# Fused chunk-select attention and soft-slot experts: longer load runs with 64 by 64 transposes, a maximum subtracted in PSUM, and combine transposes moved

## Chip, core and metric

The kernel runs on one core of one Trainium2 chip. The metric is the device time of a launch in microseconds (us). The kernel before took 165.16 us, the median of three runs (163.99 to 166.2).

## Reference

The work is an attention over selected chunks followed by a soft mixture of experts.

```python
# q, k, v: (4, 8, 768, 64) = (batch, heads, positions, head_dim), float32
k_min, k_max = min and max of k over each chunk of 32 positions      # 24 chunks
ub = sum(maximum(q * k_min, q * k_max), axis=-1)                      # bound per query and chunk
top_chunks = argsort(where(causal, ub, -1e9))[..., -6:]
scores = q @ k.T / 8, masked to the six chunks and to j <= i
attn = softmax(scores) @ v                                            # x: (3072, 512)

logits = x @ phi                                                      # 32 slots = 8 experts x 4
d = softmax of logits over the 3072 rows                              # dispatch
slot_out[e] = relu((d.T @ x)[e] @ w1[e]) @ w2[e]                      # w1 (8,512,1024), w2 (8,1024,512)
out = softmax of logits over the 32 slots @ slot_out                  # combine, (3072, 512) float32
```

## The kernel before

The 4 batches of 8 heads are worked as 16 pairs of heads (`NPAIR`). The order of the work on every engine is written out by hand: each engine runs its instructions in the order in which the program lists them. `GpSimd` issues all loads (`load`, `load_v`, `load_w`), which also convert float32 to bfloat16; `SyncE` issues the stores of the result.

A pair of heads passes through these steps. `load` (L141) brings q or k as a tile with 128 partitions; partition p holds, for each of the two heads, 6 neighbouring positions of 64 values, that is two runs of 1.5 KB of float32. `transposes` (L203) turns it with 12 TensorE matmuls against the identity: for each of the 6 positions and each head, 128 partitions by 64 columns become 64 partitions by 128 columns, head 0 on partitions 0 to 63 of PSUM and head 1 on 64 to 127. `evac_T` (L215) copies the result to SBUF on ScalarE and puts the positions back in order. From the transposed k, VectorE takes minimum and maximum per chunk (`kmin`, `kmax`); `qsplit` splits q by sign; `ubound` forms the bounds on TensorE, `select` finds the sixth largest on VectorE, and `ns_transposes` turns the selection. `scores` (L294) forms the scores of both heads, `expo` (L318) takes the exponential on ScalarE, `mask` applies the causal mask on GpSimd, and `pv` multiplies with v.

The loop over pairs (L591) mixes the steps of several pairs: in round i TensorE forms the scores of pair i, the bounds of pair i + 1, the transposes of pair i + 2, the products with v of pair i - 1, and the transposes of the finished rows of pair i - 2. Three pairs of transposes stand ahead of the loop, so 13 pairs are transposed in it. After the fourth pair of a batch the soft-slot steps for that batch follow (`moe_...`): `moe_logits` (L389), the exponentials against a running maximum over the batches, `moe_dispatch` (the slots' inputs `si`), and `moe_ct` (L506), which transposes the batch's combine weights from `c_pad` into `cT_all`.

The last batch (`BL`) is worked in the open after the loop. Its logits `lg1` lie in one PSUM tile (`lgt`). The maximum over the rows is `pm`, then transposed, reduced to `mneg` (negated) and spread over the partitions again by a small float32 product `bc` (L728). `bc` is copied to SBUF (`bc_sb`), added to the logits (`ld`), and ScalarE takes the exponential `d_sb`. `moe_dispatch(BL)` follows, and its result goes to `siT_pad`, on which the first expert layer `experts_in` waits. `keep(n)` (L687) puts n filler matmuls of 480 columns, whose results are not used, into TensorE's queue. Between the two halves of the first expert layer stands `moe_ct(BL)`. `sums` (L808) forms the slots' normaliser and the column sums of the last batch's combine weights; `inv_a` and `inv_b` hold the reciprocals that scale the output rows, `zinv` the slots' one. `experts_out` and `last_expert_out` form the second layer, the last one in two halves y (`so_sb[0]`, `so_sb[1]`). The output loop (L889) forms 12 blocks of 256 rows with five buffers: one half of a block is scaled on ScalarE, one on VectorE, and SyncE stores the block.

Of the kernel before, what the change touches and what calls it, by code (L numbers as in the profile page):

```python
# [20 lines left out]
NQT = 6  # L21
# [39 lines left out]
def kernel(  # L61
# [17 lines left out]
    SPE = NS // E  # L79
    NDG, NFG = Dm // P, F // P  # L80
    EARLY = 14
    LAST = NPAIR - 1

    ctx.enter_context(tc.manual_schedule())
# [117 lines left out]

    def transposes(i, nm):  # L203

        ps = p_tp.tile([P, NQT, P], BF16, name="tr_ps", tag="tp")
        src = st.pop((nm, i))
        for g in range(NQT):
            for h in range(2):
                nc.tensor.matmul(  # L209
                    ps[h * 64:(h + 1) * 64, g, :], lhsT=src[:, h, g * D:(g + 1) * D], rhs=ident,  # L210
                    is_transpose=True,
                )
        st[nm + "ps", i] = ps

    def evac_T(i, nm):  # L215

        t = tp3.tile([P, S], BF16, name=nm + "T", tag=nm + "T")
        nc.scalar.copy(  # L218
            t.rearrange("d (p g) -> d p g", g=NQT),
            st.pop((nm + "ps", i)).rearrange("d g p -> d p g"),  # L220
        )
        st[nm + "T", i] = t
# [163 lines left out]
        copy(st["xT", b][:, j, t0 * P:t1 * P], ps[:, t0:t1].rearrange("p t c -> p (t c)"))  # L386


    def moe_logits(b, hgs=range(NDG), ps=None, last=True):  # L389
        if ps is None:  # L390
            ps = st["lgps", b] = p_tp.tile([P, NQT, NS], F32, name="lg_ps", tag="tp")
        xT = st["xT", b]
        for t in range(NQT):
            for hg in hgs:
                nc.tensor.matmul(
                    ps[:, t, :], lhsT=xT[:, hg, t * P:(t + 1) * P], rhs=phi_sb[:, hg, :],
                    start=(hg == 0 and t == 0), stop=(last and hg == NDG - 1 and t == NQT - 1),
                )

    def moe_copy(b):  # L400
# [281 lines left out]
    normalise(LAST, 0, 3, at_a)  # L682
    pv(LAST, [4, 5])
    lgt = p_at.tile([P, 2, 512], F32, name="lgt_ps", tag="at")
    lg1 = lgt[:, 0, :NQT * NS].rearrange("p (t s) -> p t s", t=NQT)

    def keep(n):  # L687
        for _ in range(n):
            nc.tensor.matmul(h_ps[0][:, 1, CH:], lhsT=ident, rhs=w_sb[0][:, CH:512], start=True, stop=True)

    moe_logits(BL, range(NDG - 1), lg1)
    x_transposes(LAST, 0, 3)
    evac_x(LAST, 0, 3, nc.scalar.copy)
    normalise(LAST, 3, NQT, at_b)
# [3 lines left out]
    def col_sums(ps, b):  # L698
        c = cT_all[:, b * NQT:(b + 1) * NQT].rearrange("p (m a) (c x) -> p m x (a c)", a=2, x=2)
        for n in range(NQT):  # L700
            nc.tensor.matmul(
                ps[:, n:n + 1], lhsT=c[:, n // 2, n % 2], rhs=live, start=True, stop=True)

    csa = h_ps[0][:, 1, :BL * NQT]
    for b in range(BL):
        col_sums(csa[:, b * NQT:(b + 1) * NQT], b)
    moe_logits(BL, range(NDG - 1, NDG), lg1)
# [12 lines left out]
    inv_a = tail.tile([P, BL * NQT], F32, name="inv_a")  # L720
    inv_b = tail.tile([P, 1 + NQT], F32, name="inv_b")

    def cinv(n):
        return inv_a[:, n:n + 1] if n < BL * NQT else inv_b[:, 1 + n - BL * NQT:2 + n - BL * NQT]

    keep(2)
    bc = p_tp.tile([P, NS], F32, name="bc_ps", tag="tp")
    nc.tensor.matmul(  # L728
        bc, lhsT=mneg.broadcast_to([NS, P]), rhs=identf[:NS, :NS], start=True, stop=True,
    )  # L730
    rm = small.tile([P, NQT, 1], F32, name="rm", tag="rm")
    nc.vector.tensor_reduce(rm, lg1, axis=AX.X, op=ALU.max)
    nc.vector.reciprocal(inv_a, csa)
    bc_sb = small.tile([P, 1, NS], F32, name="bc_sb", tag="bc_sb")
    nc.vector.tensor_copy(bc_sb[:, 0, :], bc)
    ld = small.tile([P, NQT, NS], F32, name="ld", tag="ld")
    nc.vector.tensor_tensor(ld, lg1, bc_sb.broadcast_to([P, NQT, NS]), op=ALU.add)
    d_sb = small.tile([P, NQT, NS], BF16, name="d_sb", tag="d_sb")
    nc.scalar.activation(d_sb, ld, func=ACT.Exp)
    st["d", BL] = d_sb  # L740
    dm = small.tile([P, 1, NS], F32, name="dm", tag="dm")
    nc.vector.tensor_tensor(dm, m_old.rearrange("p (o s) -> p o s", o=1), bc_sb, op=ALU.add)
# [26 lines left out]
    for g in range(2):  # L769
# [8 lines left out]
    zinv = inv_b[:, :1]  # L778
# [29 lines left out]
    def sums():  # L808
        ps = p_tp.tile([P, 1 + NQT], F32, name="z_ps", tag="tp")
        nc.tensor.matmul(  # L810
            ps[:, :1], lhsT=zrow.rearrange("p j s -> p (j s)"), rhs=identf[:1, :1], start=True, stop=True)
        col_sums(ps[:, 1:], BL)
        nc.vector.reciprocal(inv_b, ps)

    HD = Dm // 2
# [23 lines left out]
            )  # L839

    experts_in(0, 0)
    moe_ct(B - 1)
    experts_in(0, 1)
    relu(0)
    experts_in(1, 0)
# [6 lines left out]
    def rows(m):  # L852
        return out[m * 2 * P:(m + 1) * 2 * P, :].rearrange("(p x) d -> p x d", x=2)
# [14 lines left out]
    nc.vector.tensor_scalar_mul(so_part, so_ps[:, HD:], zinv)  # L868
# [32 lines left out]


# [28 lines left out]
```

## Time and profile before

| | |
|---|---|
| median of three runs | 165.16 us |
| profiled execution | 164.61 us, span 162.9 us |
| TensorE busy | 140.9 us (86%) |
| VectorE busy | 123.3 us (76%) |
| ScalarE busy | 122.3 us (75%) |
| GpSimd busy | 103.2 us (63%) |
| HBM read, written | 52.49 MB, 6.29 MB |
| mean granted TensorE clock | 0.953 |

The profile is of one execution. Times in the timeline are in us from the start of the span. A row of the timeline has the start, the time, the engine, the line of the kernel, the operation, the tiles that it writes and reads, their shapes, and how many instructions were merged; in square brackets stands how long the engine was idle before, and what ended that. PE is TensorE's matmuls, PEld its weight loads, DVE is VectorE, ACT ScalarE, POOL GpSimd and SP SyncE. The chain is the work that ended last, followed back from the last instruction; its rows have start, time and work. The strips divide the span in 40 slices, with the busy share in tenths. Matmuls are pipelined, and their ends in the trace are modelled.

### The profile page before, as it was taken

The page shows a single profiled execution, that of the slowest core. Times are in us where ns is not written, and L with a number is a line of the kernel's source. Part 1 is how long each engine was busy: PE and PEld are TensorE (multiplying, and loading weights), DVE is VectorE, ACT ScalarE, POOL GpSimd, SP SyncE. Part 2 cuts the span into 40 slices and gives each one's busy share as a digit, 9 for nine tenths or more (in the row PEclk, how much of TensorE's full clock was granted, in tenths as well). Part 3 has the DMA queues.
Part 4 walks back from the last instruction along what each step waited for, and adds up shares of the span by engine and source line. Part 5 has one row for each costly group of instructions (what it writes and reads, how often), then busy time and mean ns, then how long its engine had stood idle before and what let it go on. Part 6 is the DMA issues. An engine that isn't in the chain of part 4 may idle for free.

```text
span 162.9 us, 5890 instructions
## 1 busy us (share of the span) xinstructions
PE 140.9 (86%) x2417; PEld 91.6 (56%) x2417; DVE 123.3 (76%) x434; ACT 122.3 (75%) x168; POOL 103.2 (63%) x203
## 2 busy tenths in 40 slices
PE   7796779999999999999999899998989899986600
PEld 2253456767767686676768567676857544442100
DVE  4466989999999999999997999898555632177620
ACT  3758879999999898999989799996986122075520
POOL 6988759989889498978959897859845400000000
PEclk9999999999999999999999999999999959999555
DMA  3999999999999999999999999999999999229996
GB/s 43 149 148 159 208 179 127 173 197 202 202 202 203 202 206 180 207 198 183 214 191 211 197 208 195 212 214 197 210 199 214 215 215 211 59 82 406 404 404 255
DMA packets 40603, 32.92 MB, mean 202 GB/s; under 512 B 26368, under 2 KB 34816, under 8 KB 40576
## 3 DMA queue, kind: packets, MB, share of 16 engines
q0 software_dynamic: 38416, 26.25, 109.2%
q1 hardware_dynamic: 2160, 6.29, 9.9%
q8 instruction: 19, 0.31, 0.7%
q14 instruction: 8, 0.07, 0.1%
HBM read 52.49 MB, written 6.29 MB: 361 GB/s over the span
## 4 chain that ended last, share of the span: by engine, by line
PE 49%; ACT 17%; DVE 11%; DMA 8%; issue 6%; POOL 4%; POOLq 0%; ACTq 0%; DVEq 0%
ACT e_sb L325 11%; PE sc_ps L301 9%; PE at_ps L353 8%; PE sc_ps L311 6%; DMA out_dram<-o_sb 5%; PE tr_ps L209 5%; PE xT_ps L375 4%; ACT qT L218 3%; PE h_ps L790 3%; DMA k_in<-in_k_dram 3%; PE ub_ps L260 2%; PE so_ps L824 2%; DVE x_sb L366 2%; PE ub_ps L253 1%; DVE mx L272 1%
## 5 line engine op out<-in xcount | busy, mean ns | idle before, releaser
L325 ACT ACTIVATE e_sb<-sc_ps 128x1024 bf16<-128x1024 f32 (+1 forms) x96 | 83.2, 917 | 7.8 <-PE sc_ps L311 7.2
L335 POOL TENSOR_SCALAR_AFFINE_SELECT e_sb<-e_sb 128x256 bf16<-128x256 bf16 x96 | 38.5, 418 | 16.1 <-ACT e_sb L325 15.6
L301 PE MATMUL sc_ps<-qT,kT 64*128 64x384 bf16 (+3 forms) x258 | 36.8, 305 | 2.5 <-ACT e_sb L325 1.6
L311 PE MATMUL sc_ps<-nsT,smask 64*128 64x384 bf16 (+2 forms) x294 | 38.1, 284 | 0.1
L353 PE MATMUL at_ps<-v_t,e_sb 128*128 128x65 bf16 x672 | 29.8, 194 | 1.7 <-DVE x_sb L366 1.3
L353 PEld LDWEIGHTS <-e_sb 128*128 128x128 bf16 x672 | 25.6, 98 | 4.0 <-issue 2.6
L301 PEld LDWEIGHTS <-kT 64*128 64x128 bf16 x258 | 13.9, 93 | 10.6 <-issue 5.3
L272 DVE MAX8 mx<-ub_ps 128x8 f32<-128x8 f32 (+1 forms) x192 | 16.8, 162 | 3.7 <-PE ub_ps L260 2.8
L311 PEld LDWEIGHTS <-smask 64*128 64x128 bf16 x294 | 14.9, 94 | 3.9 <-issue 0.6
L151 POOL DMA_DIRECT2D v_t<-in_v_dram x16 | 16.6, 1038 | 0.6 <-PE ns_ps L283 0.5
L227 DVE TENSOR_REDUCE mm<-kT 128x24 bf16<-128x768 bf16 x16 | 15.1, 944 | 2.2 <-ACT kT L218 2.2
L366 DVE TENSOR_TENSOR x_sb<-at_ps,inv 128x768 bf16<-128x768 f32 (+1 forms) x17 | 15.5, 910 | 0.6
L233 DVE TENSOR_REDUCE mm<-kT 128x24 bf16<-128x768 bf16 x16 | 15.1, 943 | 0.0
L218 ACT COPY qT<-tr_ps 128x768 bf16<-128x768 bf16 x16 | 12.8, 800 | 2.3 <-PE tr_ps L209 2.3
L218 ACT COPY kT<-tr_ps 128x768 bf16<-128x768 bf16 x16 | 12.8, 802 | 1.0 <-PE tr_ps L209 1.0
L146 POOL DMA_DIRECT2D k_in<-in_k_dram x16 | 11.8, 735 | 1.1 <-POOLq L915 0.8
L146 POOL DMA_DIRECT2D q_in<-in_q_dram x16 | 11.5, 716 | 0.0
L139 POOL DMA_DIRECT2D w_sb<-in_moe_w_dram x16 | 11.4, 712 | 0.0
L386 DVE COPY xT_sb<-xT_ps 128x768 bf16<-128x768 bf16 (+1 forms) x15 | 8.0, 537 | 2.6 <-PE xT_ps L375 2.6
L894 PE MATMUL o_ps<-so_all,cT_all 128*128 128x512 bf16 x22 | 7.5, 428 | 2.5 <-ACT o_sb L856 2.2
L247 DVE TENSOR_SCALAR qpn<-qT 128x768 bf16<-128x768 bf16 x15 | 9.2, 610 | 0.0
L209 PE MATMUL tr_ps<-ident,k_in 128*64 128x128 bf16 x192 | 8.4, 223 | 0.6 <-DMA k_in<-in_k_dram 0.5
(137 smaller groups left out, 206.3 us busy)
## 6 DMA issues: line engine op xcount, KB each, us to landing
w_sb<-in_moe_w_dram POOLq DMA_DIRECT2D x16, 1024.0 KB, 12.6
out_dram<-o_sb SPq DMA_DIRECT2D x10, 512.0 KB, 4.9
k_in<-in_k_dram POOLq DMA_DIRECT2D x16, 192.0 KB, 6.3
q_in<-in_q_dram POOLq DMA_DIRECT2D x16, 192.0 KB, 6.9
v_t<-in_v_dram POOLq DMA_DIRECT2D x16, 192.0 KB, 7.7
out_dram<-o_sb SPq DMA_DIRECT2D x2, 256.0 KB, 4.1
out_dram<-first SPq DMA_DIRECT2D x2, 128.0 KB, 2.0
out_dram<-first SPq DMA_DIRECT2D x1, 256.0 KB, 2.1
```

Of the source, the lines that this page charges most:

```text
L146: nc.gpsimd.dma_start(out=t, in_=src.rearrange("h (p g) d -> p h (g d)", p=P))
L151: nc.gpsimd.dma_start(out=v_t[i % NV][:, :, :, :D], in_=v[b, 2 * j:2 * j + 2].rearrange("h (g p) d -> p h g d", p=P),)
L209: nc.tensor.matmul(ps[h * 64:(h + 1) * 64, g, :], lhsT=src[:, h, g * D:(g + 1) * D], rhs=ident, is_transpose=True,)
L218: nc.scalar.copy(t.rearrange("d (p g) -> d p g", g=NQT), st.pop((nm + "ps", i)).rearrange("d g p -> d p g"),)
L227: nc.vector.tensor_reduce(mm[:, 0, 0, :], kT, axis=AX.X, op=ALU.min)
L272: nc.vector.max(mx[:, a, :], ub[:, a, :max(8, 4 * t + 4)])
L301: nc.tensor.matmul(ps[:, h, c:c + w], lhsT=kT[r, kg * P:(kg + 1) * P], rhs=qT[r, qs], start=True, stop=False,)
L311: nc.tensor.matmul(ps[:, h, c + (f - t0) * P:c + (l - t0) * P], lhsT=smask[r, x, kg].rearrange("p a b -> p (a b)"), rhs=nsT[r, (f - x * NJ ...
L325: nc.scalar.activation(e[:, :, :w], st.pop(("scps", i, g))[:, :, :w], func=ACT.Exp, scale=scale)
L335: nc.gpsimd.affine_select(out=e[:, :, c:c + P], in_=e[:, :, c:c + P], compare_op=ALU.is_ge, fill=0.0, base=0, pattern=[[0, 2], [1, P]], ch ...
L353: nc.tensor.matmul(o, lhsT=st["e", i, g][:, h, c:c + P], rhs=v_t[i % NV][:, h, kg, :], start=(kg == 0), stop=(kg == t),)
L366: nc.vector.tensor_tensor(st["x", b][:, t0:t1, 2 * j:2 * j + 2, :].rearrange("p t h d -> p h t d"), at[:, :, :, :D], inv.broadcast_to([P, ...
```

## The change

Three things change.

First, a load of q or k puts head 0 on partitions 0 to 63 and head 1 on 64 to 127, with 12 neighbouring positions (3 KB of float32) in a partition. The transposes become 24 matmuls of 64 partitions by 64 columns, against a 64 by 64 part of the identity; the copy to SBUF reorders 12 instead of 6 positions.

Second, the logits of the last batch are formed twice side by side (`lg12`, through a phi that is read twice). The first copy, `lg1`, serves the maxima and the combine weights. On the second, `lg2`, one float32 product adds the negated maximum in PSUM, and ScalarE takes the exponential from there. `bc_sb` and `ld` are gone; `bc` stays for `dm`. The row maximum `rm` and the reciprocal `inv_a` stand earlier on VectorE.

Third, the last `moe_ct`, the column sums and their reciprocal move into the output loop, behind block 3 (`last_rows`). `slot_sums` keeps only the slots' normaliser. The fillers after the last dispatch go from 2 to 5, and the two halves of the last expert are formed in the other order.

```diff
@@ load
-        t = inp.tile([P, 2, NQT * D], BF16, name=nm + "_in", tag=nm + "_in")
+        t = inp.tile([P, NT2 * D], BF16, name=nm + "_in", tag=nm + "_in")      # NT2 = 2 * NQT
-        nc.gpsimd.dma_start(out=t, in_=src.rearrange("h (p g) d -> p h (g d)", p=P))
+        nc.gpsimd.dma_start(out=t, in_=src.rearrange("h (p g) d -> (h p) (g d)", g=NT2))
@@ transposes
-        ps = p_tp.tile([P, NQT, P], BF16, name="tr_ps", tag="tp")
+        ps = p_tp.tile([P, NT2, 64], BF16, name="tr_ps", tag="tp")
-        for g in range(NQT):
+        for g in range(NT2):
             for h in range(2):
+                r = slice(h * 64, (h + 1) * 64)
                 nc.tensor.matmul(
-                    ps[h * 64:(h + 1) * 64, g, :], lhsT=src[:, h, g * D:(g + 1) * D], rhs=ident,
-                    is_transpose=True,
+                    ps[r, g, :], lhsT=src[r, g * D:(g + 1) * D], rhs=ident[r, r], is_transpose=True,
                 )
@@ evac_T
-            t.rearrange("d (p g) -> d p g", g=NQT),
+            t.rearrange("d (p g) -> d p g", g=NT2),
@@ moe_logits
+        else:
+            phi = phi_sb.rearrange("p g (o s) -> p g o s", o=1).broadcast_to([P, NDG, 2, NS])
...
-                    ps[:, t, :], lhsT=xT[:, hg, t * P:(t + 1) * P], rhs=phi_sb[:, hg, :],
+                    ps[:, t, :], lhsT=xT[:, hg, t * P:(t + 1) * P], rhs=phi[:, hg],
@@ after the loop
-    lg1 = lgt[:, 0, :NQT * NS].rearrange("p (t s) -> p t s", t=NQT)
+    lg12 = lgt[:, 0, :2 * NQT * NS].rearrange("p (t o s) -> p t o s", t=NQT, o=2)
+    lg1, lg2 = lg12[:, :, 0, :], lg12[:, :, 1, :]
...
+    inv_a = tail.tile([P, BL * NQT], F32, name="inv_a")
+    nc.vector.reciprocal(inv_a, csa)
...
     nc.vector.tensor_reduce(pm, lg1.rearrange("p t s -> p s t"), axis=AX.X, op=ALU.max)
+    rm = small.tile([P, NQT, 1], F32, name="rm", tag="rm")
+    nc.vector.tensor_reduce(rm, lg1, axis=AX.X, op=ALU.max)
...
     keep(2)
+    rep = identf[:NS, :NS].rearrange("p (o s) -> p o s", o=1)
+    nc.tensor.matmul(
+        lg2, lhsT=mneg.broadcast_to([NS, P]), rhs=rep.broadcast_to([NS, NQT, NS]),
+        start=False, stop=True, skip_group_check=True,
+    )
     bc = p_tp.tile([P, NS], F32, name="bc_ps", tag="tp")
...
-    nc.vector.tensor_copy(bc_sb[:, 0, :], bc)
-    nc.vector.tensor_tensor(ld, lg1, bc_sb.broadcast_to([P, NQT, NS]), op=ALU.add)
-    nc.scalar.activation(d_sb, ld, func=ACT.Exp)
+    nc.scalar.activation(d_sb, lg2, func=ACT.Exp)
...
     moe_dispatch(BL)
-    keep(2)
+    keep(5)
...
+    def slot_sums():
+        ps = p_tp.tile([P, 1], F32, name="z_ps", tag="tp")
+        nc.tensor.matmul(ps, lhsT=zrow.rearrange("p j s -> p (j s)"), rhs=identf[:1, :1], start=True, stop=True)
+        nc.vector.reciprocal(zinv, ps)
+
+    def last_rows():
+        moe_ct(BL)
+        ps = p_tp.tile([P, NQT], F32, name="cs_ps", tag="tp")
+        col_sums(ps, BL)
         nc.vector.reciprocal(inv_b, ps)
...
     experts_in(0, 0)
-    moe_ct(B - 1)
     experts_in(0, 1)
...
     hidden_T(1)
-    sums()
+    slot_sums()
...
     nc.vector.tensor_scalar_mul(so_part, so_ps[:, HD:], zinv)
+    last_expert_out(1)
+    nc.vector.scalar_tensor_tensor(so_sb[1], so_last, zinv, so_part, op0=ALU.mult, op1=ALU.add)
     last_expert_out(0)
     nc.scalar.activation(so_sb[0], so_ps[:, :HD], func=ACT.Copy, scale=zinv)
-    last_expert_out(1)
-    nc.vector.scalar_tensor_tensor(so_sb[1], so_last, zinv, so_part, op0=ALU.mult, op1=ALU.add)
@@ output loop
             nc.sync.dma_start(out=rows(m), in_=o_sb)
+        if m == 3:
+            last_rows()
```

More of the change, by code (lines that the diff above doesn't have):

```diff
@@ L81 @@
     EARLY = 14
+    NT2 = 2 * NQT
     LAST = NPAIR - 1
@@ L386, in evac_x, with moe_logits @@
         copy(st["xT", b][:, j, t0 * P:t1 * P], ps[:, t0:t1].rearrange("p t c -> p (t c)"))
-    def moe_logits(b, hgs=range(NDG), ps=None, last=True):
+    def moe_logits(b, hgs=range(NDG), ps=None):
+        phi = phi_sb
         if ps is None:
             ps = st["lgps", b] = p_tp.tile([P, NQT, NS], F32, name="lg_ps", tag="tp")
+        else:
+            phi = phi_sb.rearrange("p g (o s) -> p g o s", o=1).broadcast_to([P, NDG, 2, NS])
         xT = st["xT", b]
@@ L395, in moe_logits @@
                 nc.tensor.matmul(
-                    ps[:, t, :], lhsT=xT[:, hg, t * P:(t + 1) * P], rhs=phi_sb[:, hg, :],
-                    start=(hg == 0 and t == 0), stop=(last and hg == NDG - 1 and t == NQT - 1),
+                    ps[:, t, :], lhsT=xT[:, hg, t * P:(t + 1) * P], rhs=phi[:, hg],
+                    start=(hg == 0 and t == 0), stop=(hg == NDG - 1 and t == NQT - 1),
                 )
@@ L706 @@
         col_sums(csa[:, b * NQT:(b + 1) * NQT], b)
-    moe_logits(BL, range(NDG - 1, NDG), lg1)
+    moe_logits(BL, range(NDG - 1, NDG), lg12)
     nc.gpsimd.memset(siT_pad, 0.0)
@@ L719 @@
     nc.vector.tensor_reduce(mneg, pmT, axis=AX.X, op=ALU.max, negate=True)
-    inv_a = tail.tile([P, BL * NQT], F32, name="inv_a")
-    inv_b = tail.tile([P, 1 + NQT], F32, name="inv_b")
+    inv_b = tail.tile([P, NQT], F32, name="inv_b")
+    zinv = tail.tile([P, 1], F32, name="zinv")
     def cinv(n):
-        return inv_a[:, n:n + 1] if n < BL * NQT else inv_b[:, 1 + n - BL * NQT:2 + n - BL * NQT]
+        return inv_a[:, n:n + 1] if n < BL * NQT else inv_b[:, n - BL * NQT:n - BL * NQT + 1]
     keep(2)
+    rep = identf[:NS, :NS].rearrange("p (o s) -> p o s", o=1)
[3 more added lines that the diff above has]
+    )
     bc = p_tp.tile([P, NS], F32, name="bc_ps", tag="tp")
@@ L730 @@
     )
[L731 to L737, printed above, removed]
     d_sb = small.tile([P, NQT, NS], BF16, name="d_sb", tag="d_sb")
-    nc.scalar.activation(d_sb, ld, func=ACT.Exp)
+    nc.scalar.activation(d_sb, lg2, func=ACT.Exp)
     st["d", BL] = d_sb
     dm = small.tile([P, 1, NS], F32, name="dm", tag="dm")
-    nc.vector.tensor_tensor(dm, m_old.rearrange("p (o s) -> p o s", o=1), bc_sb, op=ALU.add)
+    nc.vector.tensor_tensor(dm[:, 0, :], m_old, bc, op=ALU.add)
     nc.scalar.activation(dm, dm, func=ACT.Exp)
@@ L806, in hidden_T @@
             nc.vector.tensor_copy(o, i_)
[L808 to L812, printed above, removed]
+    def slot_sums():
[6 more added lines that the diff above has]
+        col_sums(ps, BL)
         nc.vector.reciprocal(inv_b, ps)
```

3 lines of the change are left out of this document (1 added, 2 removed).

## Prediction

> **What bounds the kernel now.** I read the page first, then the busy time by stretch, then the chain that ended last in one steady pair, and last the timeline of the tail and of the first ten microseconds.
>
> ```profile
> PE 140.9 (86%) x2417; PEld 91.6 (56%) x2417; DVE 123.3 (76%) x434; ACT 122.3 (75%) x168; POOL 103.2 (63%) x203
> ...
> PEclk9999999999999999999999999999999959999555
> DMA  3999999999999999999999999999999999229996
> ```
>
> The page names no single bound: TensorE leads the busy times, and the DMA engines are full until slice 34. So I go to one steady pair of heads (columns: window, its length, busy time of TensorE, weight loads, VectorE, ScalarE, GpSimd, clock, DMA share, GB/s).
>
> ```profile
> 39.57:46.08 6.51, 6.42 (x128) 4.53 (x125) 6.41 (x23) 6.48 (x9) 5.26 (x12) 1.00 1.27 199
> ```
>
> A pair takes 6.5 us, and TensorE (6.42), VectorE (6.41) and ScalarE (6.48) are each busy nearly all of it. Nothing here can grow for free, and no engine can gain alone by more than the few hundredths that the others leave.
>
> ```profile
> 34.17 0.06 PE sc_ps L311 x2
> ...
> 35.08 0.46 PE tr_ps L209 x12
> 35.54 0.48 PE at_ps L353 x12
> ...
> 36.78 0.46 PE xT_ps L375 x6
> ...
> 38.06 0.70 ACT qT L218
> ```
>
> This is the chain inside the pair before it: TensorE's matmuls one after the other, then ScalarE's copy of the q transposes. The transposes lie on it. The timeline of the same pair shows how tight:
>
> ```profile
> 37.40 0.53 PE L209 MATMUL tr_ps<-ident,q_in 128*64 128x128 bf16 x12
> ...
> 37.97 0.80 ACT L218 COPY qT<-tr_ps 128x768 bf16<-128x768 bf16 x1
> ```
>
> The q transposes end at 37.93 and the copy starts at 37.97. So what the change adds to or takes from the 12 transposes counts twice per pair (k and q), as a loss in full, as a gain only to the little that ScalarE leaves.
>
> **The start: loads in runs of 3 KB.** The same bytes come in half as many packets.
>
> ```profile
> 4.32 1.47 ACT L192 COPY smask<-schunk 128x1536 bf16<-128x1536 bf16 x1 [2.23 <-DVE schunk L191]
> ...
> 4.89 0.53 PE L209 MATMUL tr_ps<-ident,k_in 128*64 128x128 bf16 x12
> ...
> 5.70 0.79 ACT L218 COPY kT<-tr_ps 128x768 bf16<-128x768 bf16 x1
> ...
> 6.63 0.53 PE L209 MATMUL tr_ps<-ident,q_in 128*64 128x128 bf16 x12 [0.46 <-DMA q_in<-in_q_dram]
> ...
> 8.22 0.53 PE L209 MATMUL tr_ps<-ident,k_in 128*64 128x128 bf16 x12 [0.52 <-DMA k_in<-in_k_dram]
> ...
> 8.55 0.35 DVE L243 TENSOR_SCALAR qpn<-qT 128x768 bf16<-128x768 bf16 x1
> ...
> 9.24 0.46 PE L260 MATMUL ub_ps<-bd,qpn 128*128 128x48 bf16 x12
> ```
>
> The first three loads land about 1.6 to 1.7 us apart (4.89, 6.63, 8.22); 192 KB in 1.65 us is 119 GB/s, while the steady pair above moves 199 GB/s. At that rate a load would take 0.99 us. Between 0.99 and 1.65 I take 1.3. An earlier first k gains nothing: its copy at 5.70 waits for the smask copy that ends at 5.79. An earlier second k lets TensorE pass to the bounds matmuls at 9.24 sooner, but these also need qpn, ready at 8.55 + 0.35 = 8.90. So the gain is at most 9.24 - 8.94 = **0.3**, which even 1.3 us per load gives (the second k would be there at about 7.5). Bounds: 0 if loads go no faster, 0.6 if the issues on GpSimd ahead of the smask copy shrink as well; a loss I exclude, since bytes and queue stay and packets halve. In the steady state no wait in the chain is for a load, so there it is worth nothing. A sentence apart: the Trainium skill (DMA: Bandwidth & Descriptors, Specifications) puts full rate at runs of 512 B or more; by it 1.5 KB runs lose nothing, and this gain would be 0; the 119 against 199 GB/s here rather speak against it.
>
> **The transposes.** Now 12 matmuls with 128 moving columns, in pairs for the two heads; 12 take 0.46 us, the same as the 6 full-width transposes of xT, so a pair runs side by side. After: 24 matmuls with 64 columns, in 12 pairs on opposite corners of the array. That row halves run side by side too is seen at L311, where two matmuls of 128 columns on 64 rows each take 0.06. If pairs stay side by side, 12 pairs of 64 columns stream as long as 6 pairs of 128. Bounds by rows: at best the block is shorter by the half-length of its last step, some 0.03. The nearest row is the one behind it, 12 matmuls of 65 columns one after the other: 0.48, that is +0.02. At worst no two overlap and each pays the pitch of the smallest matmuls,
>
> ```profile
> 52.78 0.59 PE lg_ps L395 x24
> ```
>
> 0.59 / 24 = 0.025 us; 24 of them and the end of the block that is there now (0.46 less six steps of 0.056, about 0.12) give 0.71, or **+0.25**. I take **0**, between the two near ends. The loop transposes 13 pairs, 26 tensors: 0, with near ends -0.8 and +0.5 and the far end +6.5. The copy behind them moves the same 768 elements, 0.80 us; its walk through PSUM steps 64 elements and not 128, and I take no change.
>
> **The tail: maximum in PSUM.**
>
> ```profile
> 129.04 0.40 PE L728 MATMUL bc_ps<-identf,mb 32*128 32x32 f32 x2
> ...
> 129.48 0.19 DVE L735 COPY bc_sb<-bc_ps 128x32 f32<-128x32 f32 x1
> ...
> 129.50 0.56 PE L689 MATMUL h_ps<-w_sb,ident 128*128 128x480 bf16 x2
> ...
> 129.70 0.36 DVE L737 TENSOR_TENSOR ld<-lgt_ps,bc_sb 128x192 f32<-128x192 f32 x1
> ...
> 130.15 0.36 ACT L739 ACTIVATE d_sb<-ld 128x192 bf16<-128x192 f32 x1 [2.70 <-DVE dm L742]
> ...
> 130.57 0.80 PE L486 MATMUL si_ps<-d_sb,x_sb 128*128 128x32 bf16 x24 [0.51 <-ACT d_sb L739]
> ```
>
> From the start of bc to the Exp are 1.11 us: 0.40 for bc, the copy, the addition. In their place comes one f32 product with 192 columns. No f32 matmul that wide is in the trace; bc with 32 columns takes 0.40, and its other 160 columns cost between 0.07 (at 0.056 per 128) and 0.28 (four times that). I take 0.6. The doubled logits cost some 0.1 on the way (24 matmuls going from 0.025 towards the 0.04 of the 65-column row, most of it ahead of other waits). So the Exp comes 0.4 earlier. But TensorE's queue holds bc (about 0.3) and two fillers (0.2 each) behind the new product, 129.13 + 0.45 + 0.3 + 0.4 = 130.28, and the dispatch matmuls cannot pass them: **-0.3** there, bounds -0.5 and 0. What waits for bc (dm, its Exp, the scaling of si_acc) moves later by 0.5 and still ends by 131.0, ahead of the dispatch's end. rm and inv_a now precede the maximum on VectorE, in time in which it waited for TensorE: 0.
>
> **The tail: fillers and transposes moved.**
>
> ```profile
> 130.00:131.20 1.20, 0.69 (x25) 0.63 (x24) 0.75 (x4) 1.00 (x5) 0.00 (x0) 0.79 1.07 215
> 131.20:132.30 1.10, 1.10 (x14) 0.31 (x14) 0.61 (x3) 0.00 (x0) 0.00 (x0) 0.50 1.05 212
> 133.30:134.10 0.80, 0.80 (x9) 0.02 (x2) 0.00 (x0) 0.00 (x0) 0.00 (x0) 0.50 1.04 210
> 134.10:135.00 0.90, 0.90 (x22) 0.58 (x22) 0.37 (x1) 0.00 (x0) 0.00 (x0) 1.00 1.04 209
> ```
>
> ```profile
> 131.32 1.01 PE L689 MATMUL h_ps<-w_sb,ident 128*128 128x480 bf16 x2
> ...
> 132.25 1.90 PE L790 MATMUL h_ps<-w_sb,siT_pad 128*32 128x512 bf16 x16
> ...
> 134.08 0.51 PE L509 MATMUL cT_ps<-ident,c_pad 128*128 128x128 bf16 x6
> 134.63 0.56 DVE L517 COPY cT_all<-cT_ps 128x768 bf16<-128x768 bf16 x1 [2.05 <-PE cT_ps L509]
> ...
> 135.68 0.60 ACT L797 ACTIVATE h_sb<-h_ps 128x512 bf16<-128x512 f32 x1 [4.53 <-PE h_ps L790]
> ...
> 139.21 0.30 PE L701 MATMUL z_ps<-live,cT_all 128*128 128x1 bf16 x6
> ...
> 139.55 0.20 DVE L813 RECIPROCAL inv_b<-z_ps 128x7 f32<-128x7 f32 x1 [0.26 <-PE z_ps L701]
> ```
>
> The granted clock was 0.50 from about 130.7 (0.79 on average over 130.0 to 131.2) to 134.1, so fillers took 0.4 each and the first 16 expert matmuls 1.9. Two fillers become five: +0.6 at full clock, +1.2 at half. The combine transposes leave this stretch: -0.44 at full clock. If the half clock lies where it does now, the 0.3 won before is worth half, 0.15; in full-clock terms -0.15 + 0.6 - 0.44 = **0** at the first Relu. The six column sums that follow the second hidden transposes also leave: **-0.25**. The swap of the last expert's halves I cost at nothing: the half that waits for so_part still waits for it,
>
> ```profile
> 142.80 0.40 PE L835 MATMUL so_ps<-w_sb,hT_pad 128*32 128x256 bf16 x8 [0.58 <-DVE so_part L868]
> ```
>
> and that half still feeds ScalarE's copy and the first output. The transposes, copy and sums land behind the fourth output block. There the DMA covers them:
>
> ```profile
> 145.10 3.49 DVE L859 TENSOR_SCALAR o_sb<-o_ps,inv_a 128x512 f32<-128x512 f32 x5
> ...
> 149.11 0.75 DVE L859 TENSOR_SCALAR o_sb<-o_ps,inv_a 128x512 f32<-128x512 f32 x1 [0.52 <-DMA out_dram<-o_sb]
> 150.40 0.75 DVE L859 TENSOR_SCALAR o_sb<-o_ps,inv_a 128x512 f32<-128x512 f32 x1 [0.54 <-DMA out_dram<-o_sb]
> ```
>
> VectorE is ahead of the stores by five blocks and then waits 0.5 for each. The move costs it 0.56 for the copy, 0.2 for a reciprocal and two trips to TensorE, about 1.5 in all, on the fifth block; its stores queue behind three blocks of 1.3. 0, and about +0.5 if that cover is too short.
>
> **Sum.** -0.3 (start) + 0 (transposes) + 0 (fillers) - 0.25 (sums) = -0.55. The profiled execution took 164.61 (span 162.9 and 1.7 around it), 0.55 under the median of 165.16; I take its own time: **164.1 us**.
>
> **Rivals.** *The two matmuls of a corner pair do not overlap in pace* (slower). Place: the 26 tensors of the loop. Price: +0.25 each, 6.5; 164.1 + 6.5 = 170.6. It decides from +0.17 per tensor (4.4 in all is 2% above the median). For it: L395 shows 24 matmuls of 32 columns at 0.025 each however short, and no pair in this trace runs faster than 0.056 per two. Against it: that pace is exactly what columns demand in those pairs, so it tells no floor. A sentence apart: the Trainium skill (TensorE: Matmul & The Clock Gate, Wait — 56ns, not 53.3ns?) says that start-to-start never drops below some 25 ns however few columns; if that holds across corners, this rival is the case, and the rows here cannot refute it.
>
> *The whole goes well* (faster). TensorE's pairs reach -0.03 (-0.8), the start gives 0.6 and not 0.3, and the stretch from 131 to 134 keeps full clock, because the wait ahead of the dispatch is shorter and filled. Work from the first filler to the Relu is then five fillers 1.0, a switch 0.13, two expert groups 0.85 each, 2.83 from 131.03, and 0.2 to the end: 134.1 against 135.68 now, -1.5. 164.1 - 0.8 - 0.3 - 1.5 = 161.5. For it: the half clock lasted 3.4 us and stood behind the emptiest stretch. Against: the new product changes that little.
>
> *Everything is hidden or eaten*: loads no faster, five fillers at half clock before 16 expert matmuls also at half clock (+0.6), output cover short (+0.5): 165.2 to 165.7.
>
> **Chances.** Forecast 0.36 (own range 162.6 to 165.4); faster rival 0.32, nine tenths of it under 161.9; slower rival 0.22; hidden or eaten 0.10. Two per cent is 3.3 us, about what a measurement of this kernel can tell from no change: faster 0.31, within 0.45, slower 0.24. The range 160.6 to 169.2 holds the forecast, the third rival, most of the faster one, and the slower one as far as its price is +0.2 per tensor.
>
> **What would show it.** Right: 24 transposes in 0.43 to 0.48 on the chain, pairs of 6.4 to 6.5 us, second k by 7.6, Exp of the last logits by 129.8, o_sb stores 1.3 apart through the fifth block. Wrong: transposes of 0.55 or more with pairs over 6.7; fillers of 0.4 each ahead of the experts; a gap in the stores at the moved transposes.

## The result, and the profile after

The changed kernel took 166.09 us (median of 20 runs, 165.27 to 168.66) beside 164.98 us for the kernel before on the same chip (20 runs, 163.0 to 166.2): ratio 1.0088, 95% interval 1.0062 to 1.0114. It is slower by about 1%. The medians are over all runs, while the ratios leave out the slow ones, those more than 1.5% above the fastest of their kernel. The forecast was 164.1 us. The profiled execution took 166.0 us with a span of 164.3.

The page of the changed kernel, with the rows that answer to those of before, and its row of the DMA queue that brings instructions (packets, MB, share):

```profile
PE 141.8 (86%) x2806; PEld 95.4 (58%) x2806; DVE 120.8 (73%) x433; ACT 123.2 (75%) x168; POOL 98.7 (60%) x203
...
PEclk9999999999999999999999999999999999999955
DMA  3999999999999999999999999999999999219996
...
q8 instruction: 22, 0.36, 0.8%
```

The same row of the kernel before:

```profile
q8 instruction: 19, 0.31, 0.7%
```

TensorE has 389 more matmuls, each with its weight load, so 778 more instructions. 22 packets for 0.36 MB are 16 KB each, and 3 packets more for 778 instructions are one for about 260. The DMA engines are as full as before, and the half clock of one slice ahead of the expert stage is gone.

The chain in a steady pair, for comparison with the 0.46 of before:

```profile
41.11 0.23 PE ub_ps L254
41.34 0.30 PE ub_ps L261 x12
41.63 0.50 PE tr_ps L211 x24
42.13 0.48 PE at_ps L354 x12
```

The 24 corner transposes take 0.49 to 0.50 us. That is 0.04 more for each of 26 tensors, 1.0 us in all. A second loss is new. This is the chain further on:

```profile
100.25 0.49 PE tr_ps L211 x24
100.74 0.54 PE at_ps L354 x10
101.28 0.63 issue
101.91 0.23 PE at_ps L354 x2
...
107.75 0.66 PE tr_ps L211 x24
...
112.49 0.83 ACT e_sb L326
113.32 1.07 issue
114.39 0.39 PE sc_ps L302 x2
```

TensorE's timeline names no releaser for the same stalls (in brackets the idle time and what ended it):

```profile
100.67 0.60 PE L354 MATMUL at_ps<-v_t,e_sb 128*128 128x65 bf16 x10
101.91 0.23 PE L354 MATMUL at_ps<-v_t,e_sb 128*128 128x65 bf16 x2 [0.63 <-issue]
...
112.52 0.75 PE L399 MATMUL lg_ps<-phi_sb,xT_sb 128*128 128x32 bf16 x24
114.39 0.39 PE L302 MATMUL sc_ps<-qT,kT 64*128 64x512 bf16 x2 [1.12 <-issue]
```

Ten matmuls of a row of twelve run, and the other two, which have the same operands at hand, come 0.63 late. Nothing that the profile knows held TensorE. The groups of TensorE's instructions from 20 to 126 us show the same as idle time ended by "issue" (columns: busy, mean ns, idle before and what ended it):

```profile
L302 PE MATMUL sc_ps<-qT,kT 64*128 64x384 bf16 (+3 forms) x232 | 33.3, 306 | 2.4 <-issue 1.1 <-ACT e_sb L326 0.3
L354 PE MATMUL at_ps<-v_t,e_sb 128*128 128x65 bf16 x618 | 27.9, 194 | 3.0 <-DVE x_sb L367 1.4 <-issue 0.9 <-PE tr_ps L211 0.4
```

With the stalls that lie inside a block (0.66 above, where 0.49 is usual) I count six, some 2.6 to 3 us in all; the groups of before have no such entry.

That TensorE had no instruction can be counted. Put its records (matmuls, weight loads and the few semaphore instructions) in order of start. Ahead of the first record after the stalls that end at 101.91, 108.10 and 114.39 lie 4033, 4289 and 4545 records: two steps of 256, and each number leaves 193 when it is divided by 256. All 17 stalls that the profiles of this run and of those below mark "issue" on TensorE between 16 and 136 us leave this same 193, and each ends 1.3 to 1.7 us after a 16 KB packet has ended. In the kernel before no packet between 20 and 126 us ends less than 1.8 us ahead of such a place. So TensorE stood where one packet's 256 instructions ended and the next packet had only just come.

The maximum over the last logits starts at 131.67, where before it started at 127.97. So the loop lost 3.70: about 1.0 in the blocks, the rest in these stalls.

In the start, the loads did not bring what was forecast:

```profile
4.26 0.54 POOL L147 DMA_DIRECT2D q_in<-in_q_dram  x1
...
5.08 0.85 PE L211 MATMUL tr_ps<-ident,k_in 64*64 64x64 bf16 x24
...
6.96 0.57 PE L211 MATMUL tr_ps<-ident,q_in 64*64 64x64 bf16 x24
...
8.00 0.56 PE L211 MATMUL tr_ps<-ident,k_in 64*64 64x64 bf16 x24
...
8.83 0.74 DVE L244 TENSOR_SCALAR qpn<-qT 128x768 bf16<-128x768 bf16 x1
...
9.63 0.47 PE L261 MATMUL ub_ps<-bd,qpn 128*128 128x48 bf16 x12 [0.41 <-DVE qpn L244]
```

The second k is there only 0.2 earlier, and the bounds matmuls start 0.39 later, since qpn, which they wait for, is late. The exponentials of pair 0 start 0.41 later, and pair 1 is then 0.55 shorter than before, so little of it is left either way.

In the tail, time came back:

```profile
132.74 0.59 PE L737 MATMUL lgt_ps<-identf,mb 32*128 32x192 f32 x2
...
133.42 0.33 ACT L746 ACTIVATE d_sb<-lgt_ps 128x192 bf16<-128x192 f32 x1 [2.22 <-PE lgt_ps L737]
...
133.81 0.76 PE L490 MATMUL si_ps<-d_sb,x_sb 128*128 128x32 bf16 x24
...
134.50 1.17 PE L694 MATMUL h_ps<-w_sb,ident 128*128 128x480 bf16 x5
```

From the product that brings the maximum to the Exp are 0.68 us instead of 1.11. From the start of the maximum to the end of the span are 32.63 us instead of 34.93; about 1.4 of the 2.3 is the half clock that this execution did not have, an estimate (two fillers at 0.4 instead of 0.2, the first 16 expert matmuls in 1.9 instead of 0.85).

### The profile page after: what moved, and what is told of

The parts are those of the page before. It is cut to its first block, busy times and chain, and to the rows that moved or that the text cites. A ratio compares the mean times of both kernels' runs of the same rounds, so it can differ in the third digit from the quotient of the medians.

```text
span 164.3 us, 6667 instructions
## 1 busy us (share of the span) xinstructions
PE 141.8 (86%) x2806; PEld 95.4 (58%) x2806; DVE 120.8 (73%) x433; ACT 123.2 (75%) x168; POOL 98.7 (60%) x203
## 3 DMA queue, kind: packets, MB, share of 16 engines
q0 software_dynamic: 34320, 26.25, 105.5%
q1 hardware_dynamic: 2160, 6.29, 9.5%
HBM read 52.49 MB, written 6.29 MB: 358 GB/s over the span
## 4 chain that ended last, share of the span: by engine, by line
PE 50%; ACT 18%; DVE 14%; issue 7%; DMA 3%; POOL 2%; DVEq 0%; ACTq 0%
ACT e_sb L326 12%; PE sc_ps L302 8%; PE at_ps L354 7%; PE sc_ps L312 6%; PE tr_ps L211 5%; PE xT_ps L376 4%; ACT qT L219 4%; PE warm_ps L202 3%; DMA out_dram<-o_sb 3%; PE ub_ps L261 2%; PE h_ps L796 2%; PE so_ps L834 2%; DVE x_sb L367 2%; DVE o_sb L868 2%; PE ub_ps L254 1%
## 5 line engine op out<-in xcount | busy, mean ns | idle before, releaser
L336 POOL TENSOR_SCALAR_AFFINE_SELECT e_sb<-e_sb 128x256 bf16<-128x256 bf16 x96 | 39.0, 419 | 22.2 <-ACT e_sb L326 21.3
L354 PE MATMUL at_ps<-v_t,e_sb 128*128 128x65 bf16 x672 | 30.3, 194 | 3.1 <-DVE x_sb L367 1.4
L147 POOL DMA_DIRECT2D k_in<-in_k_dram x16 | 9.2, 578 | 1.1 <-POOLq L926 0.8
L211 PE MATMUL tr_ps<-ident,k_in 64*64 64x64 bf16 x384 | 9.5, 197 | 0.0
L147 POOL DMA_DIRECT2D q_in<-in_q_dram x16 | 8.7, 544 | 0.6 <-PE tr_ps L211 0.6
L211 PE MATMUL tr_ps<-ident,q_in 64*64 64x64 bf16 x384 | 9.0, 194 | 0.0
L211 PEld LDWEIGHTS <-k_in 64*64 64x64 bf16 x384 | 7.6, 112 | 1.9 <-DMA k_in<-in_k_dram 0.8
```

Of the source, the lines that this page charges most:

```text
L147: nc.gpsimd.dma_start(out=t, in_=src.rearrange("h (p g) d -> (h p) (g d)", g=NT2))
L211: nc.tensor.matmul(ps[r, g, :], lhsT=src[r, g * D:(g + 1) * D], rhs=ident[r, r], is_transpose=True,)
L336: nc.gpsimd.affine_select(out=e[:, :, c:c + P], in_=e[:, :, c:c + P], compare_op=ALU.is_ge, fill=0.0, base=0, pattern=[[0, 2], [1, P]], ch ...
L354: nc.tensor.matmul(o, lhsT=st["e", i, g][:, h, c:c + P], rhs=v_t[i % NV][:, h, kg, :], start=(kg == 0), stop=(kg == t),)
```

## The experiments

Theory A: the 24 transposes cost 0.04 per tensor in pace, and some 2.6 us because TensorE needs its next 256 instructions sooner than they come while the DMA engines are full; the tail wins a part back. Theory B: the loss is in the loads of 3 KB. Theory C: the tail's gain is only the clock of one execution. The first four kernels each have one part of the change.

**The tail alone** (e1_tail): the diff from the doubled logits on, with the loads and transposes of before.

> Only the changes behind the loop (maximum in PSUM, five fillers, moved transposes, order of the last expert); loads and transposes as before. Theory A (the loss lies in the 24 transposes: 0.04 us more per block, 1.0 in all, and about 2.6 us in which TensorE stands without waiting for a semaphore while its instructions are refilled): this part alone wins 1 to 2.3 us, so 162.7 to 164, and no stall of TensorE without a semaphore over 0.3 us in the loop. Theory B (the loss lies in the 3 KB loads): the same, 162.7 to 164. Theory C (the tail won 2.3 us in the profile only because the clock happened to be full there): 164.5 to 165.2, no change.

Measured: 163.62 us, ratio 0.9937 (0.9899 to 0.9974). The loop is that of before to 0.15 us. The tail gains, so C in its strong form falls.

**The front alone** (e2_front): loads and transposes of the change, the old tail.

> Only the 3 KB loads and the 24 transposes per tensor; the tail as before. Theory A: 2 to 4 us slower, 167 to 169, with stalls without a semaphore of 0.3 to 1 us in the loop. Theory B: the same time. Theory C: 1 to 1.5 us slower, 166 to 166.5, since all of the measured loss is here and the tail gives nothing.

Measured: 167.04 us, ratio 1.0133 (1.0079 to 1.0187). -0.63% and +1.33% add up to +0.70%; the whole change measured +0.88%.

**The loads alone** (e3_loads): runs of 3 KB, and 12 transposes over all 128 rows, whose results mix the two heads.

```diff
-        t = inp.tile([P, 2, NQT * D], BF16, ...)
-        nc.gpsimd.dma_start(out=t, in_=src.rearrange("h (p g) d -> p h (g d)", p=P))
+        t = inp.tile([P, NT2 * D], BF16, ...)
+        nc.gpsimd.dma_start(out=t, in_=src.rearrange("h (p g) d -> (h p) (g d)", g=NT2))
```

> Only the 3 KB loads, with the 12 transposes of 128 partitions as before (the halves of the result then hold even and odd positions and not the two heads, so the selection and scores are over other data); tail as before. Theory A: 164.7 to 165.2, as before or up to 0.3 us faster, with no stall over 0.3 us. Theory B: 2 us slower or more, 167.

Measured: 163.16 us, ratio 0.9929 (0.9898 to 0.996). B is refuted: the loads by themselves gain 0.7%. That is also more than theory A gave them, and the one profiled execution (164.53) was the slowest of its runs, so its trace does not show where.

**The transposes alone** (e4_tr24): 24 corner transposes from tiles loaded in the old way; half of the positions are transposed twice and half are left out.

> Only the 24 transposes of 64 by 64 (each reads its own head's half of the partitions, and the half is written twice, so the other half of the positions is left out); loads in runs of 1.5 KB and tail as before. Theory A: as the loads with the transposes, 2 to 4 us slower, 167 to 169, blocks of 0.495 us and stalls without a semaphore. Theory B: 1.0 us slower by the blocks alone, 166, without stalls.

Measured: 169.64 us, ratio 1.0229 (1.0163 to 1.0295). The loop is 4.7 us longer, with stalls of the same kind. So the whole loss is here, and beside the old loads it is larger than beside the new ones.

**Is it the DMA engines?** Theory D, formed here, has the stalls come from the 64-row transposes themselves. In the next two kernels half of each expert weight tile is loaded and used twice, which takes 8.4 of the 26.2 MB of the loads away (26.25 to 17.86 MB on the two pages of the changed kernel); nothing else changes, and TensorE's instructions stay as many.

```diff
             dst = w_sb[i].rearrange("p (a f) -> p a f", a=NDG // 2)
+            src, dst = src[:, 0], dst[:, 0]
...
-                    rhs=w_sb[e][:, dg * F + f * 512:dg * F + (f + 1) * 512],
+                    rhs=w_sb[e][:, (dg % 2) * F + f * 512:(dg % 2) * F + (f + 1) * 512],
```

> The changed kernel, but only half of each expert weight tile is loaded and that half is used twice, so the expert outputs are computed from the wrong half of the weights; the instructions of TensorE stay as many as in the changed kernel. About 6.3 MB of transfer is gone, so that the DMA engines have room from about the middle of the loop. Theory A (TensorE runs out of instructions because their refills of 16 KB queue behind the full DMA engines): the stalls without a waiting semaphore shrink from about 3 us in the loop to under 0.8 us, the transpose blocks stay at about 0.495 us, and the kernel stands against the old kernel with the same halved weights (next run) at -1.0 (tail) +1.0 (block pace) -0.7 (loads), that is between 1.5 us faster and 0.3 us slower. Rival D (the stalls belong to the 64-row transposes themselves or to waiting loads, not to the refills): the stalls stay at 2.5 to 3.5 us and it is 1 to 2 us slower than the next run. If the weights were a bound of the end, both halved kernels would also be faster than their full ones.

> The kernel before, with only half of each expert weight tile loaded and used twice (expert outputs from the wrong half of the weights). It is the base of the run above. Theory A: the kernel before has nearly no such stalls, so relief of the DMA engines brings little: 163.5 to 165.0 us. If refills or loads cost the old kernel something too, it is 1 us or more faster than the kernel before.

Measured: 163.23 us for the changed kernel, ratio to the full kernel before 0.989 (0.9829 to 0.9952); 164.4 us for the kernel before, 0.9984 (0.9941 to 1.0027). With less to load the changed kernel is 1.2 us faster than the old one by the medians, where it was 1.1 slower with full weights. The busy times from 100 to 108 us (window, length, busy time of TensorE, weight loads, VectorE, ScalarE, GpSimd, clock, DMA share, GB/s), first of the changed kernel, then with halved weights:

```profile
100.00:108.00 8.00, 7.27 (x172) 5.26 (x168) 6.36 (x25) 7.00 (x10) 5.34 (x13) 1.00 1.31 204
```

```profile
100.00:108.00 8.00, 7.91 (x172) 5.62 (x171) 7.82 (x33) 7.85 (x11) 4.93 (x12) 1.00 1.24 176
```

The same 172 matmuls, and the 0.64 of stall is gone. The rows do not show idle DMA engines: their share falls from 1.31 to 1.24 only, the bytes from 204 to 176 GB/s. Stalls remained at 42 and 49 us, where the engines were still full with the first weights, and TensorE's wait of 0.49 that ends at 111.95 lies at a block's end too.

**Half of the added instructions** (e11_q24): the new load and 24 transposes for q alone.

> The kernel before with the new load and the 24 transposes for q alone; k is loaded and transposed as before, the tail is the old one. It has half of the added TensorE instructions. Theory A, if the refill stalls grow with the number of instructions: half of what front alone cost (ratio 1.013, +2.2 us), so 165.3 to 166.2 us. If there is a threshold (the refill arrives in time until the rate passes some value): the load's gain (half of 1.2) less 13 x 0.04 us is left, 164.2 to 164.8 us. Rival D (the stalls follow from what k's transposes or k's load do): no stalls, and 164.2 to 164.8 us as well; then the trace decides, by stalls beside q's blocks or their lack.

Measured: 164.27 us, ratio 0.9997 (0.9952 to 1.0041), no stall; the pairs are 0.04 longer as they should. This fits the case with a threshold: 20 refills instead of 19 still come in time, though five of them end only 1.2 to 1.5 us before TensorE needs them.

**The number, or the 64-row transposes?** Two kernels add instructions of another kind: 1x1 matmuls ahead of the old transposes, 12 (e16_tiny) and 24 (e17_tiny2) per tensor.

```diff
+            for y in range(2):
+                nc.tensor.matmul(one[:1, 384 + 2 * g + y:385 + 2 * g + y], lhsT=ones_sq[:, :1], rhs=ones_sq[:, :1], ...)
```

> The kernel before with 12 matmuls of 1x1 output ahead of each tensor's transposes (two ahead of each pair), as many added TensorE instructions as the change has, but no 64-row tiles and the old loads. The price of the 1x1 matmuls themselves is not known from any row; if each takes 0.02 to 0.06 us, the blocks are 0.24 to 0.72 us longer, the pairs 0.5 to 1.4 us, and the time 170 to 183 us. It is the trace that decides. Theory A (number of instructions): stalls of 0.3 us or more without a waiting semaphore appear in the loop while the DMA engines are full, some 1.5 to 3 us in all, fewer the more the pairs are stretched, since the refills then have more time. Rival D (the 64-row transposes): none of them, as in the kernel before.

> The same with 24 of the 1x1 matmuls for each tensor, twice as many added instructions as the change has. Theory A: more refills, closer together for the time they take, and as many or more stalls without a semaphore than in the run above. Rival D: none.

Measured: 206.23 and 219.51 us (one run each). They missed their aim. Each change between a 1x1 pair and a pair of transposes costs so much that two pairs come 0.30 apart instead of 0.06, pairs of heads last 9.15 us, and the refills have 40% more time: the timeline of TensorE marks no stall of this kind. Theory A's 1.5 to 3 us were missed; at that pace the runs tell A and D not apart.

The next two do it with hardly any added work: the mask matmuls of the kernel before are cut into pieces of 128 columns.

```diff
-                for h in range(2):
+                for u, h in ((u, h) for u in range(f, l) for h in range(2)):
...
-                        rhs=nsT[r, (f - x * NJ) * P:(l - x * NJ) * P], start=False, stop=(l == t1),
+                        rhs=nsT[r, (u - x * NJ) * P:(u + 1 - x * NJ) * P], start=False, stop=(u == t1 - 1),
```

> The kernel before with each mask matmul of up to 384 columns cut into pieces of 128 (the same columns, 24 more matmuls with their weight loads for each pair, about as many added instructions as the change has; no 64x64 transposes, old loads and tail). Theory A (number of instructions): stalls of 0.3 us and more without a waiting semaphore in the loop, 1.5 to 4 us in all, beside a price of the cut itself of 0 to 0.5 us a pair; 167 to 176 us, with TensorE's refills as many as after the change (22). Rival D (the stalls need the 64-row transposes): none; only the price of the cut.

> The same with halved expert weights (half of each tile loaded and used twice; expert outputs from the wrong half). Theory A: the stalls are gone or under 1 us once the first weights are in, and the run is 1.5 to 4 us faster than the one above, where halving brought the old kernel 0.3 us. Rival D: the same time as the run above within 0.5 us.

Measured: 167.42 us, ratio 1.0197 (1.0131 to 1.0263), and with halved weights 164.46, ratio 0.9995 (0.9953 to 1.0038). The chain with full weights:

```profile
55.77 0.46 PE tr_ps L209 x12
56.22 0.38 PE at_ps L353 x8
56.60 1.14 issue
57.74 0.30 PE at_ps L353 x4
```

The busy times of the same stretch, with full and then with halved weights:

```profile
52.00:60.00 8.00, 6.87 (x159) 5.52 (x155) 5.92 (x26) 6.00 (x8) 4.05 (x10) 1.00 1.33 202
```

```profile
52.00:60.00 8.00, 8.00 (x188) 6.53 (x185) 7.73 (x28) 7.08 (x11) 5.28 (x12) 1.00 0.86 102
```

Old transposes, old loads, old tail, as many more instructions as the change has (its page too shows 22 packets of instructions): the same kind of stall, and none in that stretch with DMA at 102 GB/s. That settles it for the number of instructions against the form of the transposes: the stalls need no 64-row transposes.

**What the tail's gain is made of.** Theory F: the end of the expert stage is set by TensorE's chain and the last weight tile at nearly the same time. The maximum in PSUM alone (e12_max), the late transposes, sums and order alone (e13_late), and the tail with 2 fillers instead of 5 (e7_tail_keep2):

```diff
     moe_dispatch(BL)
-    keep(5)
+    keep(2)
```

> The kernel before with the maximum subtracted in PSUM alone (second copy of the last logits, row maximum and reciprocal of the sums drawn ahead); the combine transposes, the sums, the order of the last expert halves and the filler matmuls stay as before. If the tail's gain of 1.04 us is that of the shorter path from the maximum to the exponential, 0.4 to 0.5 us of it is here (164.1 to 164.4 us) and the rest belongs to the moved transposes and sums and to the full clock; if the full clock in the first expert matmuls comes from the earlier dispatch itself, the half clock is gone here too and it is 163.3 to 163.9 us; if it comes from the three added filler matmuls, the half clock (about 3.4 us of it before) is still seen here.

> The kernel before with the late part of the tail alone: combine transposes and sums of the last batch moved into the output loop, slot sums by themselves, the other half of the last expert first; the maximum goes the old way by VectorE and the fillers stay 2. Theory F (the end of the expert stage is set by two things that come at nearly the same time, the chain on TensorE and the landing of the last weight tile; either shortened alone gains little): TensorE's chain is 0.4 to 0.7 us shorter and what it gains above some 0.3 us turns into a wait for the weights, so -0.3 to -0.6 us (ratio 0.996 to 0.998). If the order of the last halves is what pays (first output earlier by the shorter way from the weights), it has nearly the whole tail gain, -0.8 to -1.0 us, as max alone had none.

> The kernel with only the tail changed, but with 2 filler matmuls after the last dispatch as before instead of 5. If the fillers do something (keep the clock up while TensorE waits for the slots), it is 0.3 us or more slower than the tail alone (164.0 or more) and its records show a half clock in the first expert matmuls; if they do nothing, 163.4 to 163.8 us as the tail alone. The three matmuls are about 1.1 us of TensorE time: were they on the path, it would be up to 0.6 us faster, were it not for the wait for the weights that ends at the same point.

Measured: 164.76 us, ratio 1.0003 (0.9958 to 1.0048); 164.72 us, 1.0022 (0.9988 to 1.0056); 164.07 us, 0.9939 (0.9904 to 0.9974). Neither part gains alone, both together gain 0.6%, and the three added fillers do nothing. The chain of e12_max shows where its gain went:

```profile
118.06 24.15 DMA w_sb<-in_moe_w_dram
142.21 0.04 issue
142.26 0.43 PE so_ps L840 x8
```

TensorE is ready 1.8 us before that and waits for the last weight tile. In the tail alone it waits too, until 141.09. So with the old loop the weights' landing and TensorE's chain end the expert stage within 2 us of each other, and a gain in one turns into a wait for the other. With the weights halved:

> The kernel with only the tail changed and with halved expert weights (half of each tile loaded and used twice, expert outputs from the wrong half). Theory F: with the weights out of the way the whole of the tail's shorter chain is seen, and it is 1.3 to 2.0 us faster than the old kernel with halved weights (164.4), that is 162.4 to 163.1 us. Without the floor of the weights (rival): the same -1.04 us as with full weights or less. Beside the changed kernel with halved weights (163.23) it tells the price of the block pace and of the remaining stalls.

> The kernel before with only the maximum subtracted in PSUM, and with halved expert weights (expert outputs from the wrong half). With full weights this part alone gained nothing, while its TensorE chain was ready 1.8 us before the last weight tile. Theory F: with halved weights the gain of the shorter path is seen, 0.3 to 0.6 us against the old kernel with halved weights (164.4). Rival: the part gains nothing by itself, 164.2 to 164.6 us.

Measured: 162.67 us, ratio 0.9896 (0.9852 to 0.994), and 163.56 us, 0.994 (0.9903 to 0.9976), beside 0.9984 for the old kernel with halved weights. The maximum alone, worth nothing with full weights, is now worth about 0.4%, the whole tail 0.9%. The intervals are as wide as that difference, so it supports the floor rather than proves it. And the changed kernel with halved weights (0.989) equals the tail alone with halved weights (0.9896) within their intervals of half a per cent: with less to load no cost of the new loads and the 24 transposes together is seen.

A second part of the tail's gain lies behind the experts and needs no floor. These are rows of the output, from 150 to 158 us, of the kernel before, the maximum alone, the late part alone and the whole tail:

```profile
150.00:158.00 8.00, 3.01 (x7) 0.60 (x5) 3.75 (x5) 3.44 (x5) 0.00 (x0) 0.57 1.02 405
150.00:158.00 8.00, 2.19 (x5) 0.45 (x4) 3.75 (x5) 3.44 (x5) 0.00 (x0) 0.63 1.03 407
150.00:158.00 8.00, 2.65 (x7) 0.63 (x6) 3.84 (x6) 3.44 (x6) 0.00 (x0) 0.68 1.02 405
150.00:158.00 8.00, 1.34 (x4) 0.29 (x3) 3.00 (x4) 2.75 (x4) 0.00 (x0) 0.79 1.02 418
```

With the same full DMA share, the stores run at 418 to 420 GB/s in this stretch in all five kernels that have the whole tail, and at no more than 407 in the output of the others. The 6.29 MB then take some 0.5 us less, half of the 1.0 that the tail gains. So that neither part gains alone is not the floor's doing only. Why the stores go faster no run shows.

Why the weights landed 1 us sooner with the whole tail (141.1 against 142.2 with the maximum alone) is open. The half clock ahead of the experts is not settled either: it was absent in profiles with the old tail too (e11_q24, e13_late), so most of the 2.3 us of the one execution is not the change's doing; the medians give 1.0. The tail alone is faster than both kernels, and the version to keep.

**A stall without added instructions.** The profiled execution of the tail alone with halved weights (163.77, the slowest of its six) has two stalls in the loop, though its loop has the instructions of the kernel before. The first, and the row of the DMA engines before it:

```profile
109.53 0.75 PE L401 MATMUL lg_ps<-phi_sb,xT_sb 128*128 128x32 bf16 x24
111.39 0.39 PE L304 MATMUL sc_ps<-qT,kT 64*128 64x512 bf16 x2 [1.11 <-issue]
```

```profile
104.60:108.90 4.30, 4.30 (x89) 3.16 (x88) 3.78 (x18) 4.26 (x7) 2.22 (x6) 1.00 1.40 170
```

TensorE passed the end of a block of 256 at 104.59, and the packet for the block behind the next end started only at 108.87, 4.3 us later; in between the DMA share was 1.40 and 170 GB/s moved. The second stall, 0.66, ends at 119.46 in the same way. So halved weights do not keep the engines free throughout, and added instructions are not needed for a stall: they make the 256 run out sooner, as full engines make the packet come later.

## Why the prediction was wrong

**The transposes** were the step that failed. The prediction costed the edit by the pace of the array alone, took 0 and gave near ends of -0.8 and +0.5. The pace is +0.04 per tensor, 1.0 in all, outside the near ends and far under the far end of 6.5. And the step counted no cost for 778 more instructions as such: the refills behind them, with the DMA engines full on the very page that was quoted, brought 2.6 to 3 us of stalls. The loop was thus 3.7 us longer where the sum had 0.

**The slower rival** had the right sign by the wrong mechanism: corner pairs do run side by side. 12 pairs take 0.49, not 0.71. The floor of 25 ns between starts that the Trainium skill states (TensorE: Matmul & The Clock Gate, Wait — 56ns, not 53.3ns?) does not hold across two corners: 24 starts in 0.495 us, block end included, are one in 21 ns.

**The start** was put at -0.3 and gave 0. The second k came 0.2 earlier and not 0.7, and qpn was the later of the two conditions, not ready at 8.90 but at 9.57. Through the whole run the loads are nevertheless worth 0.7%, which the prediction had put at nothing.

**Maximum in PSUM**: 0.4 on the way to the Exp, as forecast (0.59 for the wide product against 0.6). **Sums and transposes moved**: the chain of the output shows them at 148.90 to 149.97, before the stores wait again at 152.56, covered as forecast: the stores run at 390 to 422 GB/s from 148 us on. Both ran into the last weight tile, which the prediction did not name as a condition of the last expert's halves; in the changed kernel the loop was late enough that it did not show. The faster stores, 0.5 us, were in no term.

**The sum**: start 0, transposes +3.7, tail -2.3 make +1.4 in the two profiled executions (164.61 and 166.0); the runs say +1.1. Of the tail's 2.3 the 1.4 of clock was the luck of one execution. The range held the time; the direction was wrong.

## What to carry to other kernels

Count instructions, not only columns: where TensorE has little slack and the DMA engines are full, 16% more instructions in the same time can cost more than their work. What to compare is the time in which TensorE runs 256 instructions and the time that the next packet of them needs; in stretches of full engines the second was 5.5 to 6.3 us here. Idle time ended by "issue" in the middle of a row of equal matmuls is the mark of it. And where two things end a stage within a microsecond or two, the gain of each alone measures nothing; try them together, or take one away.

## What the runs showed of the hardware

TensorE's instructions come in packets of 16 KB over the DMA engines, one for 256 instructions (19 packets for 4862 records in the kernel before, 22 for 5639 after the change, 25 for 6398 in e17_tiny2), and in a tight loop they can come late. In the changed kernel one such packet lies just ahead of the stall at 113.32 (the DMA queues from 111.7 to 112.8 us):

```profile
q0 software_dynamic: 59, 0.22, 100.9%
q8 instruction: 1, 0.02, 5.1%
```

The Trainium skill (Runtime: NRT & Kernel Launch, Instruction fetch mechanics) states the same block of 16 KiB, 256 instructions, and calls crossing it mostly hidden. The trace agrees with the size and, for the kernel before, with the rest; with 22 refills and full engines it is not hidden, about 2.6 us here. At the six stalls of the changed kernel the packet started 3.3 to 4.0 us after TensorE had passed the end of the block before, took 0.9 to 1.0, and 1.3 to 1.7 later TensorE went on, 5.5 to 6.3 us in all; TensorE's own work for such a block was 5.1 to 6.0 us, in the loop of the kernel before 5.5 to 7.7. Where a refill waits before its packet starts, no view shows.

Loads in half as many packets also shorten their issue on GpSimd: 0.54 to 0.58 us instead of 0.72 to 0.74 for each of the 32 loads of q and k.
